# A convolution ahead of a feed-forward: seven pairs of rounds convolved beside TensorE instead of six, and seven half tasks on GpSimd instead of four

## The chip, the cores and the metric

The kernel runs on one core of a Trainium2 chip. The metric is device time in microseconds (us) of one execution; lower is better. The engines are TensorE (PE, matrix products; PEld is its weight loads), VectorE (DVE), ScalarE (ACT), GpSimd (POOL) and SyncE (SP, which only issues transfers here).

## What is computed

The input x is 8 sequences of 3904 rows of 192 numbers. First comes a causal convolution along the sequence: 8 heads of 24 columns, 7 taps for each head, the taps a softmax of `weight`. Its result, 31232 rows, goes through a product of two linear maps and two more linear maps:

```python
out = np.einsum('hk,bskhg->bshg', w, x_unf)      # w: softmax of the taps, x_unf: 7 shifted rows
a = x @ w1                                        # (31232,192) @ (192,1024)
b = x @ w2
h = a * b @ w3                                    # (1024,1024)
return (h @ w_out).astype(np.float32)             # (1024,192)
```

## The kernel before

**Two streams and rounds.** The rows are cut into two halves of 15616 (`TS`), which are worked side by side: partitions 0 to 63 hold 64 columns of one half, 64 to 127 of the other. A half is cut into 31 rounds of 512 rows (the last has 256). The last two maps are multiplied once at the start (`w3_product`, L651), so each round has two products. The first (`first_product`, L543) makes a and b for 8 slices of 128 columns, 24 matmuls a slice (L558), reading the convolved rows transposed (columns on partitions); ACT copies a out of PSUM (`asb`, L565), and DVE multiplies it by b into `abT` (L567). The second (`second_product`, L577, once for each half) is 32 matmuls (L583), a copy by ACT (L588) and one output transfer on SP's queue (L593).

**Phases.** Rounds are taken in threes. Phase 0 has the second products of rounds 0 to 2 (their first products are the prologue); phase p from 1 to 8 has the first products of rounds 3p to 3p + 2 and then their six second products. Phase 9 takes the first products of 27 to 29, phase 10 the rest. A phase's places 0 to 5 are the points behind its six second products.

**Two ways to convolve.** Most rounds are convolved on PE. Rows are loaded in windows of 32, of which 26 come out (`conv`, L306, matmuls L324 with a band of taps, evicted by ACT or DVE at L333). Windows are gathered in blocks (`SIZES`): four in the prologue, then 40, 80, 80, 80. A block's x comes by casting loads on GpSimd's queue (L158), four for 40 windows, eight or more for 80, more where a sequence starts inside. A unit is one `conv` call over all windows of a block and part of its columns: a block of 40 is two units of 64 matmuls, a block of 80 four units of 32. `places` tells behind which second product of which phase each unit stands. With its last unit, the block is stored to DRAM (`store`, L355 and L362, on SP's queue) and read back transposed, round by round, three DMA transposes each (`transposes`, L396), into a ring of four rounds (`xT`).

The rounds of the pairs in `SIDE` are convolved beside PE. Pair p is rounds 2p + 1 and 2p + 2. For each 64 columns (a task, three to a pair) GpSimd's queue casts the rows into DRAM (`side_cast`, L440), SP's queue brings them in transposed (`side_transpose`, L450), ACT writes the tap next to the last (`side_first`, L456), and DVE adds the other six, one operation over 1024 columns each (`side_sums`, L474). Where a sequence starts inside a task, five of these six are cut in two. Two whole tasks, named in `BY_POOL`, are summed by GpSimd in halves of 512 columns instead (`pool_sums`, L501 to L521, with its own transpose, L495).

**What sets the order.** It is written out by hand, and each engine works its own instructions in order. The DVE sums are dealt over the phases by a count (`room`: 9 in phase 0, then 12) and stand behind the last `abT` of their phase, beside the second products. GpSimd's loads, casts and sums are dealt to eight `points` in the first products of a phase; each point first waits for one slice of `abT` (`pace`, L811). Each transfer on GpSimd's queue waits for the landing of the one eight places ahead of it; on SP's queue too. At the end of a phase come the transposes of rounds that are due up to two phases on; the side's transposes for the next phase stand behind the first products. Side pairs write in turn to two tiles.

Of the kernel before, what the change touches and what calls it, by code (L numbers as in the profile page):

```python
# [16 lines left out]
def kernel(  # L17
# [14 lines left out]
    G = D // H  # L32
# [6 lines left out]
    CH = 512  # L39
    NR = -(-TS // CH)  # L40
    RING = 4 * CH
    LAG = 2
    TRIO = LAG + 1
    Q = 64
    NP = D // Q
    C = 32
    ST = C - PAD
    LAG_ROWS = (LAG + 1) * CH
    SIDE = (3, 6, 7, 10, 11, 14)
    SIZES = [20, 20, 20, 40, 40, 80, 80, 80]  # L50
    NB = len(SIZES)
    FIRST = [sum(SIZES[:b]) for b in range(NB)]
    XN = 20 * D
# [359 lines left out]
    def side_span(p):  # L413
        return (2 * p + 1) * CH, min((2 * p + 3) * CH, TS)

    BY_POOL = ((7, 2), (11, 2))
    tasks = [(q, k) for q in SIDE for k in range(NP) if (q, k) not in BY_POOL]
    side_of, acc_of, raw_of = {}, [], []
    RAW = HALO + 2 * CH

# [11 lines left out]
                "p (k t) -> p k t", k=NP)  # L432

    def side_cast(i, task=None):
        p, k = task or tasks[i]
        t0, t1 = side_span(p)

        def job(r):
            def run():
                nc.gpsimd.dma_start(  # L440
                    out=rows_c[t0 - HALO:t1, k, r * Q:r * Q + Q],
                    in_=x_rows[r * TS + t0 - HALO:r * TS + t1, k * Q:k * Q + Q])
            return run
        return [job(r) for r in range(NS)]

    def side_transpose(i):
        p, k = tasks[i]
        t0, t1 = side_span(p)
        for lo, hi in ((t0 - HALO, t0 + CH), (t0 + CH, t1)):
            nc.sync.dma_start_transpose(  # L450
                out=raw_of[i % 5 - 1][:, HALO + lo - t0:HALO + hi - t0], in_=rows_c[lo:hi, k, :])

    def side_first(i):
        p, k = tasks[i]
        t0, t1 = side_span(p)
        nc.scalar.activation(  # L456
            out=acc_of[i % 2][:, 0:t1 - t0], in_=raw_of[i % 5 - 1][:, HALO - 1:HALO - 1 + t1 - t0],
            func=ACT.Copy, scale=wC[:, k, K - 2:K - 1])

    def side_sums(i):  # L460
        p, k = tasks[i]
        t0, t1 = side_span(p)
        starts = [z for z in range(0, TS, S) if t0 <= z < t1]

        def job(d, last):
            def run():
                raw, acc = raw_of[i % 5 - 1], acc_of[i % 2]
                if d == 2:
                    for z in starts:
                        nc.vector.memset(acc[:, z - t0:z - t0 + 1], 0.0)  # L470
                for lo, hi in [(t0, t1)] if last else \
                        zip([t0] + [z + d for z in starts], starts + [t1]):
                    a = acc[:, lo - t0:hi - t0]
                    nc.vector.scalar_tensor_tensor(  # L474
                        out=side_of[p][:, k, 0:t1 - t0] if last else a,
                        in0=raw[:, HALO + lo - t0 - d:HALO + hi - t0 - d],
                        scalar=wC[:, k, K - 1 - d:K - d], in1=a, op0=ALU.mult, op1=ALU.add)
# [9 lines left out]
        pool_raw.append(t[:, 2 * CH:3 * CH + HALO])  # L487

    def pool_half(p, k, half):
        lo = side_span(p)[0] + half * CH  # L490
        return p, k, lo, [z for z in range(0, TS, S) if lo <= z < lo + CH]

    def pool_transpose(p, k, half):
# [191 lines left out]
    def stage_of(R):  # L685
        return R // TRIO

    places = {0: (0, 1), 1: (0, 1, 3, 4), 2: (2, 4), 3: (1, 3), 5: (2, 4), 6: (1, 3)}
    starts, chain, room, p = {}, {}, 0, -1
    for i, (q, k) in enumerate(tasks):  # L690
        for cost, f in side_sums(i):
            while room < cost:
                p += 1
                room = 9 if p == 0 else 12
                at, ends = 0, {}
                starts.setdefault(p, [])
            if not chain or chain[max(chain)][-1][0] != i:
                starts[p].append(i)
                n = max(p == 0, -(-ends.get(i - 2, 0) // 2))
                chain.setdefault(p, []).append((i, n, lambda i=i: side_first(i)))  # L700
            assert p < stage_of(2 * q + 1)
            room, at = room - cost, at + cost
            chain.setdefault(p, []).append((i, None, f))
        ends[i] = at
    for p in starts:
        for i in starts[p]:
            assert i < 5 or p < 2 or max(v for v in chain if chain[v][0][0] <= i - 5) <= p - 2

    def side_steps(p, n, state):
        items = chain.get(p, [])  # L710
# [17 lines left out]
    def later_loads():  # L728
        nc.gpsimd.tensor_scalar(out=taps, in0=taps, scalar1=total, scalar2=None, op0=ALU.mult)
        load_x(3)  # L730
        load_wo()
        load_w3(4, 2)
        load_w3(6, 2)
        for i in starts[0]:
            for f in side_cast(i):
                f()
        load_x(4)
        for i in starts[1] + starts[2]:
            for f in side_cast(i):
                f()  # L740

# [14 lines left out]
        4: seq((w3_product, 4), (w3_product, 6),  # L756
               (conv, 3, 96, 96, (A,), (0,)), (conv, 3, 96, 96, (V,), (1,)),
               (A, wC[Q:128], wC[0:Q]), (side_tiles,), *[(side_transpose, i) for i in starts[0]],
               (store, 3), (transposes, 3))})


    units = [(b, h, n) for b in range(4, NB)
# [2 lines left out]
    assert sum(map(len, places.values())) == len(units)  # L765
    points = ((0, 1), (0, 4), (0, 7), (1, 2), (1, 5), (2, 0), (2, 3), (2, 6))
    jobs = {p: [] for p in range(1, len(phases))}
    for p, b, part in ((1, 5, 0), (1, 5, 1), (2, 6, 0), (2, 6, 1), (4, 7, 0), (5, 7, 1)):
        jobs[p] += x_jobs(b, part)
    pool_at = {2: 3, 3: 4, 4: 7, 5: 7, 6: 7}  # L770
    halves = [(q, k, h) for q, k in BY_POOL for h in range(2)]
    pool_sum = [f for v in halves for f in pool_sums(*v)]
    assert sum(pool_at.values()) == len(pool_sum)
    pool_from = {1: halves[0], 3: halves[1], 4: halves[2], 5: halves[3]}
    casts = [(p - 1, f) for p in starts if p > 2 for i in starts[p] for f in side_cast(i)]
    casts += [(p, f) for p, t in zip((1, 4), BY_POOL) for f in side_cast(None, t)]
    casts.sort(key=lambda c: c[0])
    for p in jobs:
        due_now = sum(d <= p for d, _ in casts)
# [1 line left out]
        first = [] if p == 1 else [f for _, f in casts[:due_now]]  # L781
        jobs[p] = first + jobs[p] + [f for _, f in casts[len(first):ahead]]
        del casts[:ahead]
    sent = [LAG + 2]
    due = []

    def convolve(p):
        b, h, n = units.pop(0)
        conv(b, h * G, n * G, (V, A) if p not in chain else (A, A))
        if h + n == H:  # L790
            store(b)
            while sent[0] < len(conv_rounds) and \
                    min((conv_rounds[sent[0]] + 1) * CH, TS) <= spans[b - 3][1]:
                due.append(conv_rounds[sent[0]])
                sent[0] += 1
            if p == 0:
                while stage_of(due[0]) <= 1:
                    transposes(due.pop(0))

    pace = const.tile([1, 2], BF16)  # L800
    for p, (rounds, ends) in enumerate(phases):
        todo = jobs.pop(p, [])

        each = -(-len(todo) // len(points))
        at = [[todo.pop(0) for _ in range(min(each, len(todo)))] for _ in points]
        for v in {0: (), 3: (1, 3, 5), 4: (0, 2, 4, 6), 7: range(7)}[pool_at.get(p, 0)]:
            at[v].append(pool_sum.pop(0))
# [12 lines left out]
        for b in list(zero_rows):  # L820
            for xb, p0, w in zero_rows.pop(b):
                nc.gpsimd.memset(xb[p0:p0 + PAD, w, :], 0.0)
        if p == 0:
            pool_tiles()
        for i in starts.get(p + 1, ()) if p else ():
            side_transpose(i)
        if p in pool_from:
            pool_transpose(*pool_from[p])
        state = set()
        side_steps(p, 0, state)  # L830
        for n, (R, r) in enumerate((R, r) for R in ends for r in range(NS)):
            (last_product if (R, r) == (NR - 1, NS - 1) else second_product)(R, r)
            if p == 0:
                side_steps(p, n + 1, state)
            if n in places.get(p, ()):
                convolve(p)
            side_steps(p, n + 1, state)
        assert len(state) == len(chain.get(p, ()))
        while due and stage_of(due[0]) <= p + 2:
            transposes(due.pop(0))  # L840
# [33 lines left out]
```

## Time and profile before

| what | value |
|---|---|
| median of three runs | 514.49 us (513.63 to 517.32) |
| the profiled execution | 514.11 us, of which 512.4 us span |
| `abT` on DVE (L567) | 240 of 1221 ns |
| `asb` on ACT (L565) | 244 of 1012 ns |
| sums on DVE (L474), 1024 columns | 1283 ns |
| first tap on ACT (L456), 1024 columns | 1160 ns |
| GpSimd's product (L501) and sum (L521), 512 columns | 1568 and 1266 ns |
| `ops` of a second product (L583) | 1936 matmuls, 164.0 us |
| `cps` of the convolution (L324) | 832 matmuls, 10.8 us |
| x loads on GpSimd's queue, 240 KB | 28, 7.4 us to landing |
| casts on GpSimd's queue, 130 KB | 30, 6.9 us to landing |

Busy times are sums over one execution and overlap between engines. Matmuls on PE are pipelined, four or two of them side by side on parts of the array, so their times added up exceed what they take; the chain of work gives what a group takes. The view of DMA queues calls GpSimd's queue q0 and SP's q1; both feed the same 16 DMA engines.

### The profile page before, as it was taken

The numbers are of one execution on the slowest core, as the hardware profiler recorded it, in microseconds if no ns is written. First come the engines' busy times: TensorE is split into PE (matmuls) and PEld (weight loads), VectorE is DVE, ScalarE is ACT, GpSimd is POOL, SyncE is SP. The second block draws the span as 40 slices with busy tenths as digits, with TensorE's granted clock in tenths as the row PEclk, the third lists the DMA queues.
The fourth block names the chain that finished last, engine by engine and source line by source line (L and its number), as shares of the span: only waits on it lengthen the run. The fifth ranks groups of instructions, "written<-read, shape, count | busy, mean of one in ns | idle before, by whom it ended". The sixth has DMA issues, their size and how long they took to land.

```text
span 512.4 us, 13886 instructions
## 1 busy us (share of the span) xinstructions
PE 506.9 (99%) x5892; PEld 341.0 (67%) x5892; DVE 432.5 (84%) x430; ACT 351.6 (69%) x397; POOL 161.4 (31%) x232
## 2 busy tenths in 40 slices
PE   9999999999999999999999999999999999999997
PEld 4446875496569557855875596569557845874597
DVE  7798779997999899999999998999899899339930
ACT  6786757778775876777657757776776477357742
POOL 9876004201750364069408911960000000000000
PEclk9999999999999999999999999999999999999999
DMA  9999979997999565799659534404841420230025
GB/s 142 146 170 161 166 176 195 179 174 140 178 153 204 107 50 33 178 175 161 105 146 136 65 107 101 47 11 133 156 84 33 152 66 0 71 117 1 1 64 155
DMA packets 154134, 59.45 MB, mean 116 GB/s; under 512 B 108891, under 2 KB 154071, under 8 KB 154071
## 3 DMA queue, kind: packets, MB, share of 16 engines
q1 hardware_dynamic: 86999, 41.39, 37.8%
q0 software_dynamic: 66912, 17.07, 36.5%
q8 instruction: 46, 0.75, 0.6%
q14 instruction: 17, 0.14, 0.1%
q10 hardware_dynamic: 160, 0.10, 0.1%
HBM read 34.42 MB, written 34.88 MB: 135 GB/s over the span
## 4 chain that ended last, share of the span: by engine, by line
PE 94%; ACT 2%; POOL 1%; DMA 1%; DVE 1%; issue 1%; ACTq 0%; POOLq 0%
PE ops L583 31%; PE pa L558 30%; PE pb L558 30%; DMA xb<-in_x_dram 1%; PE cps L324 1%; PE wps L651 1%; ACT convo L333 1%; ACT asb L565 1%; DVE abT L567 0%; ACT acc L456 0%; POOL xb L158 0%; PE ops L604 0%; POOL wn L226 0%; POOL wn L227 0%; POOL wn L228 0%
## 5 line engine op out<-in xcount | busy, mean ns | idle before, releaser
L567 DVE TENSOR_TENSOR abT<-asb,pb 128x1024 bf16<-128x1024 bf16 x240 | 292.7, 1221 | 50.6 <-ACT asb L565 35.1
L565 ACT CAST asb<-pa 128x1024 bf16<-128x1024 f32 x244 | 247.0, 1012 | 64.3 <-PE pa L558 63.9
L558 PEld LDWEIGHTS <-wn 64*128 64x128 bf16 x1488 | 138.5, 94 | 79.8 <-issue 1.4
L558 PEld LDWEIGHTS <-ws 64*128 64x128 bf16 x1488 | 129.5, 94 | 69.3 <-issue 1.6
L583 PE MATMUL ops<-W_sb,abT 128*128 128x192 bf16 x1936 | 164.0, 246 | 0.2 <-ACT convo L333 0.2
L583 PEld LDWEIGHTS <-abT 128*128 128x128 bf16 x1936 | 158.5, 98 | 6.7 <-issue 6.6
L558 PE MATMUL pb<-xT,wn 64*128 64x512 bf16 x456 | 124.4, 376 | 0.0
L558 PE MATMUL pa<-xT,wn 64*128 64x512 bf16 x456 | 123.1, 376 | 0.2
L558 PE MATMUL pa<-xT,ws 64*128 64x512 bf16 x456 | 123.1, 376 | 0.0
L558 PE MATMUL pb<-xT,ws 64*128 64x512 bf16 x456 | 121.1, 376 | 0.0
L588 ACT COPY osb<-ops 128x768 f32<-128x768 f32 (+1 forms) x61 | 48.5, 795 | 84.0 <-PE ops L583 82.2
L474 DVE SCALAR_TENSOR_TENSOR acc<-raw,wC,acc 128x320 f32<-128x320 bf16 (+4 forms) x90 | 76.2, 894 | 0.7
L558 PE MATMUL pb<-side,wn 64*128 64x512 bf16 (+1 forms) x288 | 75.7, 367 | 0.0
L558 PE MATMUL pa<-side,ws 64*128 64x512 bf16 (+1 forms) x288 | 74.4, 367 | 0.0
L558 PE MATMUL pa<-side,wn 64*128 64x512 bf16 (+1 forms) x288 | 74.4, 367 | 0.0
L558 PE MATMUL pb<-side,ws 64*128 64x512 bf16 (+1 forms) x288 | 72.9, 367 | 0.0
L811 POOL COPY pace<-abT 1x2 bf16<-1x2 bf16 x44 | 7.7, 174 | 159.2 <-DVE abT L567 159.1
L501 POOL TENSOR_SCALAR tmp<-acc,wC 128x512 f32<-128x512 bf16 x24 | 37.6, 1568 | 0.8
L333 ACT CAST convo<-cps 128x640 bf16<-128x640 f32 (+2 forms) x58 | 33.8, 661 | 2.1 <-PE cps L324 2.1
L158 POOL DMA_DIRECT2D xb<-in_x_dram x46 | 31.0, 677 | 4.1 <-issue 3.5
L440 POOL DMA_DIRECT2D rows_c<-in_x_dram x36 | 28.1, 783 | 9.5 <-issue 4.1
L521 POOL TENSOR_TENSOR acc<-acc,tmp 128x512 f32<-128x512 f32 (+6 forms) x25 | 26.0, 1047 | 1.7
(72 smaller groups left out, 172.4 us busy)
## 6 DMA issues: line engine op xcount, KB each, us to landing
out_dram<-osb SPq DMA_DIRECT2D x54, 384.0 KB
xb<-in_x_dram POOLq DMA_DIRECT2D x28, 240.0 KB, 7.4
rows_c<-in_x_dram POOLq DMA_DIRECT2D x30, 130.0 KB, 6.9
out_dram<-osb SPq DMA_DIRECT2D x12, 192.0 KB
rows<-convo SPq DMA_DIRECT2D x9, 240.0 KB
xb<-in_x_dram POOLq DMA_DIRECT2D x8, 228.0 KB, 8.0
rows<-convo SPq DMA_DIRECT2D x9, 150.0 KB
w3b<-in_moe_w_dram POOLq DMA_DIRECT2D x4, 256.0 KB, 5.6
```

The costliest lines, as they stand in the source:

```text
L158: nc.gpsimd.dma_start(out=tiles[js[0]][0][group(r, e), s:s + w, :], in_=bass.AP(tensor=x.tensor, offset=(r * TS + t - PAD) * D, ap=[[D, C] ...
L333: f(out=convo[:, e::E, k, :, lo:lo + c] .rearrange("p w r g -> p r w g"), in_=src[:, :, :, o:o + c])
L440: nc.gpsimd.dma_start(out=rows_c[t0 - HALO:t1, k, r * Q:r * Q + Q], in_=x_rows[r * TS + t0 - HALO:r * TS + t1, k * Q:k * Q + Q])
L474: nc.vector.scalar_tensor_tensor(out=side_of[p][:, k, 0:t1 - t0] if last else a, in0=raw[:, HALO + lo - t0 - d:HALO + hi - t0 - d], scalar ...
L501: nc.gpsimd.tensor_scalar(out=out, in0=pool_raw[0][:, HALO - d:HALO - d + CH], scalar1=wC[:, k, K - 1 - d:K - d], scalar2=None, op0=ALU.mult)
L521: nc.gpsimd.tensor_tensor(out=a, in0=a, in1=tmp[:, lo - t0:hi - t0], op=ALU.add)
L558: nc.tensor.matmul(p[:, r, f * N:f * N + N], w_of(i, k, r)[rs, ft * 128:(ft + 1) * 128], operand(R, k, rs), start=(k == 0), stop=(k == NP ...
L565: nc.scalar.copy(out=asb[:, :, 0:per * N], in_=pa[:, :, 0:per * N])
L567: nc.vector.tensor_tensor(out=ab[:, f0, :, 0:N], in0=asb[:, :, 0:N], in1=pb[:, :, 0:N], op=ALU.mult)
L583: nc.tensor.matmul(ops[:, g // 2, (g % 2) * D:(g % 2) * D + D], ab[:, jt, r, g * 128:(g + 1) * 128], W_sb[:, jt, :], start=(jt == 0), stop ...
L588: nc.scalar.copy(out=osb.rearrange("p (a g) d -> p a (g d)", g=2), in_=ops[:, 0:ng // 2, 0:2 * D])
L811: P(out=pace, in_=abT_of[R][0:1, ft, 1, 0:2])
```

## The change

The pairs beside PE become 4, 5, 8, 9, 12, 13 and 14 in place of 3, 6, 7, 10, 11 and 14: seven pairs, 14 rounds. The blocks after the prologue are three of 80. The first of them (rounds 5 to 8) is convolved in phase 0, at places 1 to 4, the second (rounds 13 to 16) in phases 2 and 3, the third (rounds 21 to 24) in phases 4 and 5. Sequence starts now lie in rounds that PE convolves, so no task is cut in two, and loads of x are. Seven half tasks go to GpSimd, one in each of phases 2 to 8; a task may keep half on DVE. DVE's counts become 9, four times 11, four times 12, and its sums reach into phase 8. In phase 0 the two first taps of ACT stand at places 1 and 4, no longer both at 1. All x of the first block of 80 is loaded in the prologue, ahead of four casts; before, it was a block of 40 ahead of eight. The transposes of round 4 move up behind those of round 3, and `turn` sends the transposes of a round once the round that held its place in the ring has been read. Outside phase 0 it is called before the side's transposes and at the end of the phase. PE's matmuls for the two products are the same; its convolution has 704 matmuls.

```diff
-    SIDE = (3, 6, 7, 10, 11, 14)
-    SIZES = [20, 20, 20, 40, 40, 80, 80, 80]
+    SIDE = (4, 5, 8, 9, 12, 13, 14)
+    SIZES = [20, 20, 20, 40, 80, 80, 80]
...
-    BY_POOL = ((7, 2), (11, 2))
-    tasks = [(q, k) for q in SIDE for k in range(NP) if (q, k) not in BY_POOL]
+    BY_POOL = ((5, 2, 0), (5, 2, 1), (8, 2, 0), (8, 2, 1), (12, 2, 0), (12, 2, 1), (13, 2, 0))
+    tasks = []
+    for q in SIDE:
+        for k in range(NP):
+            left = [h for h in range(2) if (q, k, h) not in BY_POOL]
+            if left:
+                tasks.append((q, k, half_of(q, left[0])[0], half_of(q, left[-1])[1]))
...
-    places = {0: (0, 1), 1: (0, 1, 3, 4), 2: (2, 4), 3: (1, 3), 5: (2, 4), 6: (1, 3)}
+    places = {0: (1, 2, 3, 4), 2: (1, 3), 3: (0, 1), 4: (2, 4), 5: (1, 3)}
+    rooms = (9, 11, 11, 11, 11, 12, 12, 12, 12)
...
-                room = 9 if p == 0 else 12
+                room = rooms[p]
...
-                n = max(p == 0, -(-ends.get(i - 2, 0) // 2))
+                n = max((p == 0) * (3 * len(starts[p]) - 2), -(-ends.get(i - 2, 0) // 2))
...
         load_x(4)
-        for i in starts[1] + starts[2]:
+        for i in starts[1]:
             for f in side_cast(i):
                 f()
...
-               (store, 3), (transposes, 3))})
+               (store, 3), (transposes, 3), (transposes, 4))})
...
-    for p, b, part in ((1, 5, 0), (1, 5, 1), (2, 6, 0), (2, 6, 1), (4, 7, 0), (5, 7, 1)):
+    for p, b, part in ((1, 5, 0), (2, 5, 1), (3, 6, 0), (4, 6, 1)):
         jobs[p] += x_jobs(b, part)
...
+    pool_from = {p: v for p, v in enumerate(BY_POOL, 1)}
+    pool_sum = {p + 1: pool_sums(*v) for p, v in pool_from.items()}
...
-    sent = [LAG + 2]
+    sent = [LAG + 3]
...
-        conv(b, h * G, n * G, (V, A) if p not in chain else (A, A))
+        conv(b, h * G, n * G, (V, A) if p not in chain or (p == 0 and h == 2 * n) else (A, A))
...
+    def turn(p):
+        while due and stage_of(due[0]) <= p + 2 and \
+                stage_of(conv_rounds[ring_of[due[0]] - RING // CH]) <= p:
+            transposes(due.pop(0))
...
-        for i in starts.get(p + 1, ()) if p else ():
-            side_transpose(i)
+        turn(p)
+        raws = starts.get(p + 1, ())
+        late = [i for i in raws if p == 0 or i >= 5 and chain[p][0][0] <= i - 5]
+        for i in raws:
+            if i not in late:
+                side_transpose(i)
...
-        while due and stage_of(due[0]) <= p + 2:
-            transposes(due.pop(0))
-        for i in starts[1] if p == 0 else ():
+        turn(p)
+        for i in late:
             side_transpose(i)
```

More of the change, by code (lines that the diff above doesn't have):

```diff
@@ L414, in side_span, with half_of @@
         return (2 * p + 1) * CH, min((2 * p + 3) * CH, TS)
-    BY_POOL = ((7, 2), (11, 2))
-    tasks = [(q, k) for q in SIDE for k in range(NP) if (q, k) not in BY_POOL]
+    def half_of(q, h):
+        t0, t1 = side_span(q)
+        return t0 + h * CH, min(t0 + h * CH + CH, t1)
+    BY_POOL = ((5, 2, 0), (5, 2, 1), (8, 2, 0), (8, 2, 1), (12, 2, 0), (12, 2, 1), (13, 2, 0))
[5 more added lines that the diff above has]
+                tasks.append((q, k, half_of(q, left[0])[0], half_of(q, left[-1])[1]))
     side_of, acc_of, raw_of = {}, [], []
@@ L434, in side_cast @@
     def side_cast(i, task=None):
-        p, k = task or tasks[i]
-        t0, t1 = side_span(p)
+        p, k, t0, t1 = task or tasks[i]
         def job(r):
@@ L446, in side_transpose @@
     def side_transpose(i):
-        p, k = tasks[i]
-        t0, t1 = side_span(p)
-        for lo, hi in ((t0 - HALO, t0 + CH), (t0 + CH, t1)):
+        p, k, t0, t1 = tasks[i]
+        for lo, hi in ((t0 - HALO, t0 + CH), (t0 + CH, t1))[:1 + (t1 - t0 > CH)]:
             nc.sync.dma_start_transpose(
@@ L453, in side_first @@
     def side_first(i):
-        p, k = tasks[i]
-        t0, t1 = side_span(p)
+        p, k, t0, t1 = tasks[i]
         nc.scalar.activation(
@@ L460, in side_sums @@
     def side_sums(i):
-        p, k = tasks[i]
-        t0, t1 = side_span(p)
+        p, k, t0, t1 = tasks[i]
         starts = [z for z in range(0, TS, S) if t0 <= z < t1]
+        o = t0 - side_span(p)[0]
         def job(d, last):
@@ L474, in run @@
                     nc.vector.scalar_tensor_tensor(
-                        out=side_of[p][:, k, 0:t1 - t0] if last else a,
+                        out=side_of[p][:, k, o:o + t1 - t0] if last else a,
                         in0=raw[:, HALO + lo - t0 - d:HALO + hi - t0 - d],
@@ L489, in pool_half @@
     def pool_half(p, k, half):
-        lo = side_span(p)[0] + half * CH
+        lo = half_of(p, half)[0]
         return p, k, lo, [z for z in range(0, TS, S) if lo <= z < lo + CH]
@@ L686, in stage_of @@
         return R // TRIO
-    places = {0: (0, 1), 1: (0, 1, 3, 4), 2: (2, 4), 3: (1, 3), 5: (2, 4), 6: (1, 3)}
+    places = {0: (1, 2, 3, 4), 2: (1, 3), 3: (0, 1), 4: (2, 4), 5: (1, 3)}
+    rooms = (9, 11, 11, 11, 11, 12, 12, 12, 12)
     starts, chain, room, p = {}, {}, 0, -1
-    for i, (q, k) in enumerate(tasks):
+    for i, (q, *_) in enumerate(tasks):
         for cost, f in side_sums(i):
@@ L706 @@
         for i in starts[p]:
-            assert i < 5 or p < 2 or max(v for v in chain if chain[v][0][0] <= i - 5) <= p - 2
+            assert i < 5 or p < 2 or max(v for v in chain if chain[v][0][0] <= i - 5) <= p - 1
     def side_steps(p, n, state):
@@ L767 @@
     jobs = {p: [] for p in range(1, len(phases))}
-    for p, b, part in ((1, 5, 0), (1, 5, 1), (2, 6, 0), (2, 6, 1), (4, 7, 0), (5, 7, 1)):
+    for p, b, part in ((1, 5, 0), (2, 5, 1), (3, 6, 0), (4, 6, 1)):
         jobs[p] += x_jobs(b, part)
[L770 to L776, printed above, removed]
+    pool_from = {p: v for p, v in enumerate(BY_POOL, 1)}
+    pool_sum = {p + 1: pool_sums(*v) for p, v in pool_from.items()}
+    casts = [(p - 1, f) for p in starts if p > 1 for i in starts[p] for f in side_cast(i)]
+    casts += [(p, f) for p, (q, k, h) in pool_from.items()
+              for f in side_cast(None, (q, k, *half_of(q, h)))]
     casts.sort(key=lambda c: c[0])
@@ L796, in convolve @@
             if p == 0:
-                while stage_of(due[0]) <= 1:
-                    transposes(due.pop(0))
+                turn(0)
+    def turn(p):
+        while due and stage_of(due[0]) <= p + 2 and \
+                stage_of(conv_rounds[ring_of[due[0]] - RING // CH]) <= p:
+            transposes(due.pop(0))
     pace = const.tile([1, 2], BF16)
@@ L805 @@
         at = [[todo.pop(0) for _ in range(min(each, len(todo)))] for _ in points]
-        for v in {0: (), 3: (1, 3, 5), 4: (0, 2, 4, 6), 7: range(7)}[pool_at.get(p, 0)]:
-            at[v].append(pool_sum.pop(0))
+        for v, f in enumerate(pool_sum.pop(p, ())):
+            at[v].append(f)
         def issue(R, ft, fs):
@@ L832 @@
             (last_product if (R, r) == (NR - 1, NS - 1) else second_product)(R, r)
-            if p == 0:
-                side_steps(p, n + 1, state)
             if n in places.get(p, ()):
@@ L838 @@
         assert len(state) == len(chain.get(p, ()))
-        while due and stage_of(due[0]) <= p + 2:
-            transposes(due.pop(0))
-        for i in starts[1] if p == 0 else ():
+        turn(p)
+        for i in late:
             side_transpose(i)
```

## The prediction

> **What bounds the kernel now.** I read the page first, then busy time by stretch, then the chain of work, then the queues. TensorE (PE) is busy 506.9 of 512.4 us:
>
> ```profile
> PE 506.9 (99%) x5892; PEld 341.0 (67%) x5892; DVE 432.5 (84%) x430; ACT 351.6 (69%) x397; POOL 161.4 (31%) x232
> ```
>
> By stretches of 10 us it loses time only before 70 us; from there each shows 10.00 of 10.00, at a granted clock of 1.00. So time goes where PE work goes, and comes where PE is made to wait. The chain over phase 1 prices a unit of a block of 80 (32 matmuls): 0.35 us between second products.
>
> ```profile
> 105.17 0.35 PE cps L324 x32
> 105.53 2.75 PE ops L583 x32
> 108.27 0.35 PE cps L324 x32
> ...
> 120.21 0.75 PE pa L558 x6
> ```
>
> Phases start in the chain at 71.24, 120.21, 168.33, 216.44, 263.63, 311.74, 359.85, 407.04 and 454.18. Phases without units (263.63 less 216.44, 407.04 less 359.85) take 47.19, with two 48.11, with four 48.97: a unit costs 0.46 all in, and phases are rigid.
>
> In phase 0 ScalarE's two first taps stand before the evictions of the 40-block's units, and PE waits:
>
> ```profile
> 56.34 1.11 ACT acc L456
> 57.50 1.15 ACT acc L456
> 58.65 1.83 ACT convo L333 x4
> ```
>
> GpSimd's queue, by time, at the loads of block 4 and the casts behind them:
>
> ```profile
> 39.06 2.72 POOL L158 DMA_DIRECT2D xb<-in_x_dram  x4 [1.19 <-issue]
> ...
> 49.85 0.76 POOL L440 DMA_DIRECT2D rows_c<-in_x_dram  x1 [1.55 <-DMA xb<-in_x_dram]
> 52.18 0.76 POOL L440 DMA_DIRECT2D rows_c<-in_x_dram  x1 [1.56 <-DMA xb<-in_x_dram]
> ```
>
> The last casts each wait for the landing of the DMA eight places ahead. SP's queue, where a block of 80 goes to DRAM and back transposed (columns: start, us, ...):
>
> ```profile
> 356.69 10.40 SPq L362 DMA_DIRECT2D rows<-convo  x8
> 367.14 0.90 SPq L355 DMA_DIRECT2D rows<-convo  x1
> 368.13 1.74 SPq L593 DMA_DIRECT2D out_dram<-osb  x2
> 369.97 9.05 SPq L396 DMA_TRANSPOSE xT<-rows  x6
> ```
>
> Storing 80 windows takes 11.4 us on an otherwise quiet queue. The DMA view of 136 to 142 us and of 78.5 to 81 us shows what GpSimd's loads (q0) do to SP's (q1):
>
> ```profile
> q0 software_dynamic: 1165, 0.43, 79.0%
> q1 hardware_dynamic: 1651, 0.43, 74.8%
> ```
>
> and
>
> ```profile
> q0 software_dynamic: 1050, 0.40, 140.5%
> q1 hardware_dynamic: 30, 0.01, 1.7%
> ```
>
> **The sum, part by part**, against the profiled execution (514.11 us: its span and 1.7 around it, which stay; 0.4 below the median of 514.49).
>
> (a) Units after 71 us: twelve become eight, four in phase 1 gone: 4 x 0.46 = -1.8.
>
> (b) Phase 0: 52.79 to 71.24 is 18.45: six second products at 2.69 (5.39 for two) are 16.14, two units at 0.67 are 1.34, waits 0.97. After: 16.14 + 4 x 0.46 = 17.98, since the two first taps are now at places 1 and 4, with a unit's evictions (about 1.9) and one result copy (0.80) inside 3.15 us of PE each, as phase 1 shows without a wait. -0.5. Phase 1 then starts at 70.8.
>
> (c) Block 4 is 80 windows: twelve x loads for four, with eight places between each and the one it waits for, so the last is issued at 52.2, where the last cast was. Its convolution comes after two second products, at 52.79 + 5.4 = 58.2. A 168 KB load lands 3.9 us after issue when alone (DMA issues), that cast 12.9 after: ends 56.1 and 65.1, a wait of 0 to 6.9. The rows are the same, the queue ahead is 0.8 MB, so the median of block 4's loads (7.5) is nearer above and 3.9 below: about 58.2 with the edge memset, wait 0.5. It folds into (d): what PE waits here, round 5 needn't.
>
> (d) Round 5 (its xT comes from block 4) is PE's third in phase 1: 70.8 + 2 x 10.36 = 91.5. Block 4's last eviction ends at 52.79 + 5 x 2.69 + 4 x 0.46 + 2.24 = 70.3 (2.24 from 117.46 to 119.70, unit to store, in phase 1), and SP has round 4's transposes and five outputs ahead. Low end: the quiet row, 356.69 to three transposes issued at about 374.9 less 1.7 for outputs, 16.5 + 1 to land (estimate; the shortest x load takes 2.0 with its issue): 87.8, no wait. High end: six transposes end at 59.09 + 2 x 4.49 = 68.1, five outputs at 1.37 (0.75 MB in 2.7 us) end at 75.0; then the contended row, 119.70 to the third transpose's last packets at 142, less one output, plus 1: 22 more, 97: a wait of 5.4. Block 5's loads are issued at the points where before's were (76.6, 80.1), so q1 meets the second DMA row above; I lean to the high end: (c)+(d) = +3.0.
>
> By the Trainium skill, DMA: Bandwidth & Descriptors, section Queues, rings and completion order, each DMA engine takes turns between queue rows packet by packet. The second DMA row (1050 packets to 30, with transposes issued and waiting) disagrees; by the rule SP would lose half of those 2.5 us, and (d) would be 1.8.
>
> (e) Round 13 (block 5) is PE's second in phase 4, at P4 + 10.4 (P4: that phase's start). Block 5's last unit is at place 1 of phase 3, whose unit ends 37.4 after the phase's start (108.62 less 71.24); + 2.24, so its store begins at P4 - 8.5 (48.11 less 39.6). Behind it SP has four outputs (two in the quiet row), then round 13's three transposes. Quiet: 18.2 + 2 x 1.37 + 1 = 21.9: P4 + 13.4, a wait of 3.0. Contended: 22.3 + 3 x 1.37 + 1 = 27.4: P4 + 18.9, a wait of 8.5. Casts in phase 4 reach the queue at about P4 + 7, as at 127 us, so the store is quiet and outputs and transposes are not: +5.5. Before, no block had this deadline: the one stored in phase 1 was first read in phase 3.
>
> Costed at nothing: vector sums 9, 11 to 12 a phase at 1.285, without splits (15.4, where chains of 15.96 ended 1.58 into the next phase without loss); the halves on GpSimd (18.5 us of sums a phase, beside first products, as in phases 4 to 6); the larger phase 8 chain (16 x 1.02 = 16.3), beside 16.1 of second products; its cover gone, each would cost its excess. One cast in phase 1 waits for a late transpose; nothing else of that phase is behind it on GpSimd.
>
> The Trainium skill, SBUF — State Buffer, section Who interferes with whom, has a vector operation with two SBUF inputs blocked by a GpSimd operation that reads SBUF. That would bind where GpSimd's last sums overlap the vector sums. The products that GpSimd mostly runs beside have one PSUM input and show no effect: 21 in 24.58 us with GpSimd busy 21.4 of 26, and in 24.59 with it idle. One blocked operation of 1.57 us stays within the slack above, so the sum is the same; a row of them is in the last rival.
>
> Sum: 514.1 - 1.8 - 0.5 + 3.0 + 5.5 = **520.3 us**, 1.1% over the median.
>
> **Rivals.**
> 1. *The transposed rows arrive in time* and the convolution's saving is what is left: 514.1 - 2.3 = 511.8. This decides if store, outputs and transposes together take under 18.9 us for round 13. For: no transposed operand is waited for over 0.2 us now. Against: the quiet row alone has 21.9.
> 2. *Only round 13 is late*, round 5 slips through: 511.8 + 0.5 + 5.5 = 517.8. For: from 70 to 80 us the DMA engines move only 118 GB/s, so there is room. Against: the outputs moved ahead of the store fill it.
> 3. *Both at their contended ends*: 511.8 + 5.4 + 8.5 = 525.7.
> 4. *Phase 0 waits for x as long as the last cast took* (6.9), or GpSimd's halves hold up vector sums in each of seven phases (up to 1.57 each, 11): with (e), 522 to 528.
>
> **How the numbers follow.** Forecast 0.40 (518.5 to 522.5), rivals 0.15, 0.25, 0.12, 0.08. The range of 513.0 to 525.5 leaves out most of rival 1 and half of rivals 3 and 4, about 0.2. About 1% is what a measurement here can tell from no change: slower means above 519.6, faster below 509.3. Above 519.6: three quarters of the forecast's case (0.30), rival 3, most of 4, a tenth of 2: 0.50. Faster 0.03, for a gain no row shows; the rest, 0.47, within 1%.
>
> **What would show it.** PE waits in only three places past 52 us: at the first unit of phase 0 (for x loads or the memset), at round 5 and at round 13 (for xT); phases 1, 6, 7 and 8 without these 47.2 long, phases 2, 3 and 5 48.1. PE's convolution has 704 matmuls, not 832. I'm wrong if phase 4 is 48.1 long, or if SP's round 13 transposes are issued before P4 + 5.

## The result

The changed kernel takes 539.78 us (median; 539.59 to 540.27), the kernel before 514.26 beside it (513.63 to 517.32): 4.8% slower, ratio 1.0483, 95% interval 1.0457 to 1.0510. The forecast was 520.3, its range ended at 525.5. The profiled execution has a span of 538.2 us.

The page of the changed kernel, busy time and the row of the granted clock (40 slices of 13.5 us):

```profile
PE 512.4 (95%) x5764; PEld 342.5 (64%) x5764; DVE 444.7 (83%) x396; ACT 348.8 (65%) x389; POOL 230.6 (43%) x301
...
PEclk9999889789999999996999999999999999999999
```

PE's share falls from 99% to 95%, and three dents stand in a clock that was 1.00 throughout before. The matmuls are 128 fewer, as the diff says (704 of the convolution for 832).

Phases read from PE's instructions, before, as forecast, and after:

| phase | before | forecast | after |
|---|---|---|---|
| 0 (second products) | 18.4 | 18.0 + 0.5 | 25.1 |
| 1 | 48.97 | 47.2 + 2.5 | 58.0 |
| 4 | 48.1 | 48.1 + 5.5 | 58.1 |
| 2, 3, 5 | 48.1, 48.1, 48.1 | 48.1 each | 48.1 each |
| 6, 7 | 47.2 each | 47.2 each | 47.2 each |

All of the loss is in the three phases that were named. 511.8 (the sum with nothing late) + 7.1 + 10.8 + 10.0 = 539.7. The waits of the changed kernel (us in total, times, longest) name what is late:

```profile
POOL rows_c L448 <- DMA raw<-rows_c: 16.6, 1, 16.6
PE pa L564 <- DMA xT<-rows: 16.0, 3, 8.6
...
ACT acc L462 <- DMA side<-rows_c: 7.4, 1, 7.4
...
PE cps L324 <- ACT osb L594: 4.4, 1, 4.4
```

PE's 16.0 are rounds 5 and 13. Its 4.4 stand at the second unit of phase 0, and they are not for x: the last x load had landed at 57.45, and the first unit ran at 57.97 without a wait.

```profile
57.97 0.43 PE L324 MATMUL cps<-xb,Aband 32*32 32x240 bf16 x32
58.33 2.81 PE L589 MATMUL ops<-W_sb,abT 128*128 128x192 bf16 x32
65.51 0.38 PE L324 MATMUL cps<-xb,Aband 32*32 32x240 bf16 x2 [4.37 <-ACT osb L594]
```

ScalarE's first tap waits 7.4 for a transpose, and the copy of the second result, which frees PE's bank, is behind it:

```profile
55.44 0.80 ACT L594 COPY osb<-ops 128x768 f32<-128x768 f32 x1 [2.58 <-PE ops L589]
63.63 1.15 ACT L462 ACTIVATE acc<-side,wC 128x1024 f32<-128x1024 bf16 x1 [7.39 <-DMA side<-rows_c]
64.68 0.78 ACT L594 COPY osb<-ops 128x768 f32<-128x768 f32 x1
```

The chain leads from that tap back to a cast on GpSimd:

```profile
53.05 2.30 POOL rows_c L448 x3
55.35 5.55 DMA rows_c<-in_x_dram
...
60.96 2.56 DMA side<-rows_c
...
63.63 1.15 ACT acc L462
```

Pairs 4 and 5 are now neighbours. The cast for the first task of pair 5 writes the 16 halo rows ahead of its span, and these are the last 16 rows that the second transpose of pair 4's first task reads, in the same DRAM tensor `rows_c`. (Both pairs' casts write the same values into these rows, so the order changes nothing but the time.) That cast stands behind block 4's twelve x loads and lands at 60.9, so SP, which issues in order, stands still from 45.4 to 60.9. Its queue by time:

```profile
44.12 17.96 SPq L457 DMA_TRANSPOSE side<-rows_c  x2
62.20 2.50 SPq L457 DMA_TRANSPOSE raw<-rows_c  x2
64.80 4.93 SPq L362 DMA_DIRECT2D rows<-convo  x8
...
70.34 8.68 SPq L396 DMA_TRANSPOSE xT<-rows  x6
79.06 4.45 SPq L599 DMA_DIRECT2D out_dram<-osb  x5
83.61 10.40 SPq L362 DMA_DIRECT2D rows<-convo  x6
```

Block 3's store, the transposes of rounds 3 and 4 and five results are pushed back with it, and block 4's store is first issued at 83.61, where the forecast had 75.0 at the contended end. Its last row leaves SP at 99.46, round 5's first transpose at 100.11.

Round 13, on the other hand, is as forecast in kind. The store, its results and its transposes:

```profile
223.48 7.69 SPq L362 DMA_DIRECT2D rows<-convo  x6
...
235.04 1.40 SPq L355 DMA_DIRECT2D rows<-convo  x1
236.54 4.25 SPq L599 DMA_DIRECT2D out_dram<-osb  x4
240.89 10.09 SPq L396 DMA_TRANSPOSE xT<-rows  x6
```

Phase 4 starts at 231.85: the store begins 8.4 ahead (forecast 8.5) and takes 13.0 where the quiet row had 11.4, the four results 4.25 (two in the quiet row and two at 1.37 make 4.5), and PE goes on with the last of the three transposes at 250.9, 10.0 after the first was issued. No cast runs beside the store, since GpSimd issues its first one of the phase at 236.57; casts run beside the results and the transposes.

What was not foreseen is the clock. Windows of the changed kernel around the three waits (us from the start: length, then busy time and instructions of PE, PEld, DVE, ACT and POOL, PEclk, DMA share, GB/s):

```profile
63.60:70.20 6.60, 3.97 (x51) 3.14 (x51) 5.25 (x5) 6.10 (x9) 0.00 (x0) 0.50 0.73 132
101.00:111.20 10.20, 4.08 (x20) 1.59 (x22) 1.11 (x1) 1.01 (x1) 0.00 (x0) 0.50 1.23 160
244.40:254.60 10.20, 4.83 (x22) 1.77 (x24) 1.22 (x1) 1.54 (x2) 5.17 (x6) 0.50 1.29 160
```

PE's clock is halved 2.0 to 2.5 us after each pause begins and stays halved until after work is back: 4.8 (4.1 without the gaps in it), 4.2 and 3.8 us at half speed. By this, about 2.0, 2.1 and 1.9 us are lost (an estimate: half of the work in these stretches).

### The profile page after: what moved, and what is told of

Same layout as the page of the kernel before. It is cut to its first block, busy times and chain, and to the rows that moved or that the text cites. A ratio compares the mean times of both kernels' runs of the same rounds, so it can differ in the third digit from the quotient of the medians.

```text
span 538.2 us, 13687 instructions
## 1 busy us (share of the span) xinstructions
PE 512.4 (95%) x5764; PEld 342.5 (64%) x5764; DVE 444.7 (83%) x396; ACT 348.8 (65%) x389; POOL 230.6 (43%) x301
## 4 chain that ended last, share of the span: by engine, by line
PE 77%; DMA 11%; POOL 4%; DVE 3%; SPq 1%; ACT 1%; issue 1%; POOLq 0%; ACTq 0%; DVEq 0%
PE ops L589 26%; PE pa L564 25%; PE pb L564 25%; DMA xb<-in_x_dram 3%; DVE acc L480 2%; DMA rows_c<-in_x_dram 2%; DMA xT<-rows 2%; DMA rows<-convo 2%; POOL xb L158 1%; POOL ws L220 1%; POOL w3b L638 1%; DMA wn<-in_moe_w_dram 1%; SPq L362 1%; PE cps L324 1%; SPq L396 1%
## 5 line engine op out<-in xcount | busy, mean ns | idle before, releaser
L564 PEld LDWEIGHTS <-wn 64*128 64x128 bf16 x1488 | 138.9, 95 | 96.1 <-DMA xT<-rows 15.9
L564 PE MATMUL pb<-xT,wn 64*128 64x512 bf16 x408 | 113.6, 381 | 0.0
L564 PE MATMUL pb<-xT,ws 64*128 64x512 bf16 x408 | 110.3, 381 | 0.1
L564 PE MATMUL pb<-side,wn 64*128 64x512 bf16 (+1 forms) x336 | 88.9, 368 | 0.1
L564 PE MATMUL pa<-side,wn 64*128 64x512 bf16 (+1 forms) x336 | 87.3, 369 | 0.0
L564 PE MATMUL pa<-side,ws 64*128 64x512 bf16 (+1 forms) x336 | 87.3, 369 | 0.0
L480 DVE SCALAR_TENSOR_TENSOR acc<-raw,wC,acc 128x1024 f32<-128x1024 bf16 (+2 forms) x70 | 85.1, 1216 | 2.5 <-ACT acc L462 0.5
L564 PE MATMUL pb<-side,ws 64*128 64x512 bf16 (+1 forms) x336 | 85.6, 368 | 0.0
L507 POOL TENSOR_SCALAR tmp<-acc,wC 128x512 f32<-128x512 bf16 x42 | 65.9, 1568 | 1.2
L448 POOL DMA_DIRECT2D rows_c<-in_x_dram x50 | 38.0, 763 | 22.2 <-DMA raw<-rows_c 16.6
L527 POOL TENSOR_TENSOR acc<-acc,tmp 128x512 f32<-128x512 f32 x35 | 44.4, 1268 | 2.9
L480 DVE SCALAR_TENSOR_TENSOR acc<-side,wC,acc 128x1024 f32<-128x1024 bf16 (+1 forms) x20 | 25.2, 1261 | 11.2 <-ACT acc L462 10.7
```

What stands on the lines that cost most here:

```text
L448: nc.gpsimd.dma_start(out=rows_c[t0 - HALO:t1, k, r * Q:r * Q + Q], in_=x_rows[r * TS + t0 - HALO:r * TS + t1, k * Q:k * Q + Q])
L480: nc.vector.scalar_tensor_tensor(out=side_of[p][:, k, o:o + t1 - t0] if last else a, in0=raw[:, HALO + lo - t0 - d:HALO + hi - t0 - d], sc ...
L507: nc.gpsimd.tensor_scalar(out=out, in0=pool_raw[0][:, HALO - d:HALO - d + CH], scalar1=wC[:, k, K - 1 - d:K - d], scalar2=None, op0=ALU.mult)
L527: nc.gpsimd.tensor_tensor(out=a, in0=a, in1=tmp[:, lo - t0:hi - t0], op=ALU.add)
L564: nc.tensor.matmul(p[:, r, f * N:f * N + N], w_of(i, k, r)[rs, ft * 128:(ft + 1) * 128], operand(R, k, rs), start=(k == 0), stop=(k == NP ...
```

## The experiments

Phase lengths of each kernel, from its profiled execution, beside its measured ratio to the kernel before:

| kernel | median us | ratio, 95% interval | phase 0 | phase 1 | phase 4 |
|---|---|---|---|---|---|
| after | 539.78 | 1.0457 to 1.0510 | 25.1 | 58.0 | 58.1 |
| e1_two_tensors | 533.05 | 1.0285 to 1.0373 | 25.0 | 51.5 | 58.5 |
| e2_block5_early | 529.27 | 1.0213 to 1.0297 | 24.6 | 58.4 | 48.1 |
| e3_both | 524.05 | 1.0126 to 1.0198 | 25.6 | 51.5 | 48.1 |
| e4_casts_first | 535.00 | 1.0345 to 1.0443 | 28.3 | 49.2 | 58.4 |
| e5_fill13 | 537.04 | 1.0364 to 1.0486 | 24.8 | 58.1 | 55.9 |
| e6_store_late | 524.50 | 1.0125 to 1.0210 | 20.7 | 55.2 | 48.1 |
| e7_loads_late | 519.09 | 1.0048 to 1.0097 | 26.1 | 47.1 | 48.1 |
| e8_both_late | 525.28 | 1.0148 to 1.0240 | 18.9 | 58.5 | 48.1 |
| e9_freed | 524.71 | 1.0147 to 1.0228 | 25.2 | 53.9 | 48.1 |
| e10_freed_early | 523.57 | 1.0090 to 1.0214 | 22.2 | 53.3 | 48.1 |
| e11_in_time | 519.64 | 1.0045 to 1.0103 | 25.4 | 47.1 | 48.1 |

**e1_two_tensors**: the shared halo rows taken away.

```diff
-    rows_c = dram.tile([TS, NP, NS * Q], BF16, name="rows_c")
+    rows_2 = [dram.tile([TS, NP, NS * Q], BF16, name=f"rows_c{i}") for i in range(2)]
...
+    def rows_of(q):
+        return rows_2[SIDE.index(q) % 2]
...
```

> The side pairs' rows go to two DRAM tensors, taken in turn, so that the casts of pair 5 no longer share 16 halo rows with the transposes of pair 4; nothing else moves. Theory (the second transpose of task 0 waits for the casts of pair 5 behind twelve x loads, and holds ScalarE's first tap and all of SP's queue): phase 0 is 18 to 19.5 long instead of 25.1, GpSimd's wait of 16.6 and the tap's wait of 7.4 are gone, round 5's xT comes 3 to 9 us earlier; phase 4 stays at 58. Total 521 to 529. Rival (block 4's x loads are what is late): phase 0 stays at 24 to 25, total within 2 us of 539.8. Rival (SP's queue is long in any case): phase 0 is short, but round 5's wait moves with it and stays at 9 or more, total 531 to 534.

6.7 us came back; the theory had 11 to 19 (521 to 529). GpSimd's wait of 16.6, ScalarE's of 7.4 and SP's standstill are gone, and block 4's store moves from 83.61 to 77.34:

```profile
43.45 2.52 SPq L460 DMA_TRANSPOSE side<-rows_c  x2
46.67 3.15 SPq L460 DMA_TRANSPOSE raw<-rows_c  x2
49.99 7.84 SPq L362 DMA_DIRECT2D rows<-convo  x8
...
60.40 8.16 SPq L396 DMA_TRANSPOSE xT<-rows  x6
68.60 7.39 SPq L602 DMA_DIRECT2D out_dram<-osb  x5
77.34 7.84 SPq L362 DMA_DIRECT2D rows<-convo  x6
```

Phase 1 is 6.4 shorter. But phase 0 is as long as it was, as the first rival had it (the total is in the range of the second, which had expected a short phase 0). One wait has made room for another: with SP's queue at work again, the last x load lands at 63.36 instead of 57.45, and PE's first unit now waits for x itself:

```profile
PE cps L324 <- DMA xb<-in_x_dram: 3.5, 2, 2.0
```

**e2_block5_early**: the last units of block 5 moved to phase 2.

```diff
-    places = {0: (1, 2, 3, 4), 2: (1, 3), 3: (0, 1), 4: (2, 4), 5: (1, 3)}
+    places = {0: (1, 2, 3, 4), 2: (0, 1, 3, 4), 4: (2, 4), 5: (1, 3)}
```

> The last two units of block 5 move from phase 3 to phase 2, so that its store and the transposes of round 13 are issued a phase earlier; phase 0 is as in the changed kernel. Theory (round 13's xT was late because the store stands 8.5 us before phase 4, behind it outputs and casts): phase 4 is 48.1 long instead of 58.1 and its clock stays at 1.0, phase 2 is 49.0, phase 3 47.2: total 529.5 to 531. Rival (the transposes are slow beside other transfers wherever they stand): PE still waits over 2 us for xT in phase 4, total 533 or more.

As the theory said, and a little better: 529.27, phase 4 at 48.1 and phase 2 at 49.3. Of PE's waits for xT one is left, 9.0. Term (e) was about the deadline: a phase earlier, the same store and transposes are in time.

**e3_both**: the two edits together.

> Both edits: two DRAM tensors and block 5 convolved in phase 2. Theory: the two gains add up (phase 0 and round 5: 11 to 18; phase 4: 10): total 512 to 519; 512 if round 5's xT comes in time, which would be the rival of the prediction that all transposes come in time. Rival (the waits hide each other): total over 521.

524.05: over 521, as the rival had it, but not for its reason. The gains nearly add up (10.5 and 6.7 make 17.2, measured 15.7); the first is smaller than the theory had it, since phase 0 stays. The DMA queues from 50 to 57 us show what x now shares the engines with. In the changed kernel, where SP stands still:

```profile
q0 software_dynamic: 3930, 1.17, 158.2%
q1 hardware_dynamic: 98, 0.02, 2.4%
```

and in e3_both, where SP transposes and stores beside:

```profile
q0 software_dynamic: 1737, 0.63, 84.2%
q1 hardware_dynamic: 1795, 0.45, 63.8%
```

(packets, MB, time as a share of the span of 16 engines). GpSimd's queue moves 0.63 MB in place of 1.17, and the last x load lands at 63.94 instead of 57.45, issued 1.2 later.

**e4_casts_first**: the casts ahead of the x loads, halo rows still shared.

```diff
-        load_x(4)
         for i in starts[1]:
             for f in side_cast(i):
                 f()
+        load_x(4)
```

> GpSimd issues the casts of phase 1's side tasks ahead of block 4's twelve x loads instead of behind them; the shared halo rows stay. Theory (the late casts are the cause): the second transpose of task 0 issues 6 to 9 us earlier, phase 0 gets 3 to 6 shorter, although x comes 3 to 5 us later, round 5's wait shrinks as much, phase 4 stays at 58: total 526 to 534. Rival (the x loads are what PE waits for): the same loads come later, so the first unit waits longer and the total is 540 to 545.

535.00, between the two. Phase 0 went the rival's way (28.3, 3.2 longer, PE's first unit waits for x), phase 1 the theory's (49.2, 8.8 shorter). SP's second transpose was issued at 48.67 instead of 60.96, and the last x load landed at 63.66 instead of 57.45. So both accounts hold, each in its phase.

**e5_fill13**: matmuls of zeros in the wait for round 13.

```diff
+            if R == 13:
+                warm(28)
             first_product(R, {ft: issue(R, ft, at[v])
```

> The changed kernel with 28 matmuls of zeros (128x512, no result used) ahead of round 13's first product, where TensorE waits 6.7 us; they fill 6.0 us at full clock. Theory (TensorE's pause lowers the granted clock to 0.5 for 10.24 us, and the part of it that outlasts the wait costs about 2): the clock in phase 4 stays at 1.0, xT comes no earlier, phase 4 goes from 58.1 to 55.5 to 56.7, total 537 to 538.5. Rival (the clock is no cost, or the wait alone sets the phase's end): phase 4 within 0.5 of 58.1, total within 0.7 of 539.8; or longer, if the filling matmuls outlast the wait.

The windows of the kernel with the filling:

```profile
240.00:244.00 4.00, 4.00 (x31) 1.82 (x28) 3.78 (x4) 2.42 (x3) 3.43 (x5) 1.00 1.63 274
244.00:248.00 4.00, 4.00 (x20) 1.84 (x19) 0.24 (x1) 0.00 (x0) 3.89 (x6) 1.00 2.23 192
248.00:252.00 4.00, 2.87 (x22) 1.06 (x22) 0.00 (x0) 0.92 (x1) 1.82 (x2) 1.00 1.51 199
252.00:256.00 4.00, 4.00 (x40) 2.11 (x38) 3.66 (x3) 3.13 (x4) 0.00 (x1) 1.00 0.64 82
```

The clock stays at 1.00, round 13's product starts as late as before, and phase 4 is 55.9: 2.3 less. The interval of the whole time (ratio 1.0364 to 1.0486) is too wide to show so little; the phase shows it. So this wait costs its length and about 2 more. For the other two waits that is read from the rows of the clock alone, without a run that fills them.

**e6_store_late, e7_loads_late, e8_both_late**: on e3_both, block 3's store with the transposes of rounds 3 and 4 moved behind phase 0's first result (e6), phase 1's loads and casts issued at the last 5 of 8 points only (e7), and both (e8).

```diff
-               (A, wC[Q:128], wC[0:Q]), (side_tiles,), *[(side_transpose, i) for i in starts[0]],
-               (store, 3), (transposes, 3), (transposes, 4))})
+               (A, wC[Q:128], wC[0:Q]), (side_tiles,), *[(side_transpose, i) for i in starts[0]])})
...
+            if (p, n) == (0, 0):
+                store(3)
+                transposes(3)
+                transposes(4)
...
-        each = -(-len(todo) // len(points))
+        free = range(3 if p == 1 else 0, len(points))
+        each = -(-len(todo) // len(free))
```

> Two tensors and block 5 in phase 2, and block 3's store with the transposes of rounds 3 and 4 issued behind the first result of phase 0 instead of ahead of it, so that SP's queue is quiet until about 56 us. Theory (with the shared rows gone, block 4's x loads share the DMA engines with SP's store and transposes and land at 63.9 instead of 57.5; phase 0 waits for that): the last x load lands at 57 to 59, phase 0 is 18 to 20 instead of 25.6, unless round 3's own xT is then late by up to 3; round 5's wait stays at 3 to 6 with its clock: total 516 to 521. Rival (x is late by its own bytes, or by the casts): last x load lands after 62, total within 2 of 524.

> Two tensors and block 5 in phase 2, and GpSimd's x loads and casts of phase 1 issued from the second round's middle on (5 of the 8 points) instead of from the first round on. Theory (block 4's store and round 5's transposes are stretched by those loads): the store, 12.9 us long from its first issue, takes 10 to 11.5, round 5's wait of about 2.7 with its half clock shrinks, phase 1 goes from 51.5 to 48 to 50, unless phase 2's first taps or units are then late; phase 0 stays at 25 to 26: total 520.5 to 523. Rival (SP's own queue is the length): store 12.5 or more, total within 1 of 524.

> The two edits together. Theory: phase 0 18 to 20, phase 1 48 to 51, all others as they are: total 513 to 518, near the kernel before. Rival (moved transfers collide with those behind them, as the first tap did with the x loads): over 520.

e6: phase 0 falls from 25.6 to 20.7 and the last x load lands at 60.98, the theory's way but short of its 57 to 59, and the total doesn't move (524.50, the rival's): phase 1 gives it all back. e8 is the clearest of the set. Its phase 0 is 18.9, as its theory had it and near the forecast's 18.5, but its phase 1 is 58.5, as long as without any edit, and its total is the rival's (525.28). SP's queue in e8:

```profile
56.77 6.39 SPq L362 DMA_DIRECT2D rows<-convo  x8
...
65.08 8.18 SPq L396 DMA_TRANSPOSE xT<-rows  x6
73.31 3.24 SPq L602 DMA_DIRECT2D out_dram<-osb  x4
76.64 9.21 SPq L362 DMA_DIRECT2D rows<-convo  x6
...
90.28 11.13 SPq L396 DMA_TRANSPOSE xT<-rows  x6
```

Block 4's store is first issued at 76.64 here, at 77.44 in e6, at 77.34 in e1 and 77.72 in e3, wherever phase 0 ended; round 5 waits from there. So in these four phases 0 and 1 together take 75.9 to 77.3, while phase 0 alone goes from 18.9 to 25.6. The equal times have two causes. In e1 and e3 SP is free and waits for the eviction of block 4's last unit, which late x has put back. In e6 and e8 x is earlier, but SP's queue is full: the store and transposes that the edit put behind the first result, and four results after them, take SP until 76.55 in e8.

SP issues nothing from 50 to 56 us in e6, but its queue isn't quiet on the DMA engines: the four side transposes issued before move nearly as much there as all of SP's transfers did in e3_both. From 50 to 57 us, e6:

```profile
q0 software_dynamic: 1728, 0.63, 85.2%
q1 hardware_dynamic: 1745, 0.42, 62.8%
```

In the changed kernel only the first of these four could run ahead of 61 us.

e7 came out better than its theory: round 5's wait vanishes, phase 1 is 47.1, the total 519.09. The store is hardly shorter (12.0 for 12.8, where 10 to 11.5 was expected), and SP issues round 5's first transpose no earlier (90.39 for 90.58 in e3); it is their landing that GpSimd's loads had held up: e3's PE goes on with the last at 102.1, e7's needs them from 99.5 and doesn't wait. In e8 the same edit doesn't help: phase 1 starts 7.3 earlier there than in e7, so PE needs round 5 earlier, and GpSimd's loads, tied to the first products, start at 88.11 and run beside round 5's transposes. In e7 they start at 95.43, when the third of these is being issued.

**e9_freed, e10_freed_early, e11_in_time**: the casts for phase 1's tasks issued in phase 1 (e9, e10), and phase 0's results sent to DRAM only behind block 4's store and the transposes of rounds 5 and 6 (all three; in e11 all but the first, and the casts where they were). In e9 and e10, with no result ahead of it, block 3's store is issued at about 50; in e11 it waits for the first result. The main lines of e9's edit:

```diff
+            if R < TRIO:
+                held.append((out[t0:t0 + n * 128, :], osb[:, g:g + n, :]))
+                continue
...
-    casts = [(p - 1, f) for p in starts if p > 1 for i in starts[p] for f in side_cast(i)]
+    casts = [(p - 1, f) for p in starts if p > 0 for i in starts[p] for f in side_cast(i)]
```

> The kernel with both late edits (block 3's store behind phase 0's first result, phase 1's loads late), and two things taken out of the way of block 4: the casts for phase 1's side tasks are issued in phase 1 instead of behind block 4's x loads, and phase 0's six results go to DRAM behind block 4's store and the transposes of rounds 5 and 6 instead of between. Theory (block 4 passes x load, store and transposes one after another, and what stands in SP's queue and on the DMA engines beside it makes round 5's xT late; in the kernel with both late edits the store was first issued at 76.6, 5 after phase 0's end): store from 70 to 73.5, round 5's wait from 9.9 to 0 to 4, phase 0 18 to 19.5, phase 1 47.2 to 53, total 512.5 to 518. Rival (block 4's own bytes take that long whatever is beside them): round 5's xT comes no more than 2 us earlier, total over 521.

> The same two things taken away, but block 3's store ahead of phase 0's results, as in the changed kernel, so that it runs beside the x loads. Theory: with the casts gone the x loads land at 58 to 61 instead of 64, phase 0 is 18.5 to 22 instead of 26; block 4's store starts at 70 to 75, so round 5's wait is 0 to 4: total 513 to 518. Rival (store 3 and the transposes are what slow x, not the casts): phase 0 stays at 25 to 26, and total at 518 to 520.

> The kernel with both late edits, whose phase 0 was 18.9 long but whose round 5 waited 9.9 because SP issued block 4's store only at 76.6; now five of phase 0's six results go to DRAM behind block 4's store and the transposes of rounds 5 and 6, and the casts stay in the prologue. Theory (block 4's way is a chain of x loads, store and transposes; each stretch of it that runs without company on SP's queue and on the DMA engines is short enough, none of them beside another is): x lands near 59, the store is first issued at 73 to 74 and takes 12.3, round 5's third transpose is issued by 89 to 90.5, its wait is 0 to 2.5, phase 1 47.2 to 51, total 513 to 517, as the kernel before or up to 0.5% over it. Rival (the deferred results or the transposes behind them make a new wait in phase 1's second products, as the late casts did): phase 1 over 51.5, total over 518.

In none of the three does PE wait for round 5, but all miss the totals of their theories and none beats the kernel before. e9 (524.71) and e10 (523.57) run into a new wait: the casts now come late for the taps of phase 1. The waits of e9:

```profile
ACT acc L465 <- DMA raw<-rows_c: 12.8, 2, 12.5
```

This holds ScalarE's result copies, and PE its second products (4.1, and the clock after it). e9 also shows the store alone: GpSimd's queue moves nothing from 77 to 89 us, and from 77.18 to 89.39 it takes 12.2 us. With 11.4 in the kernel before and 13.0 for block 5 in the changed kernel, a store beside which GpSimd's queue moves nothing takes 11.4 to 13.0; e3's 12.8 is no more than that, e8's 13.6 and the changed kernel's 15.9 are. Its place in the queue counts for more. In e11 (519.64) round 5 is in time and the casts too, but x lands at 62.67, phase 0 is 25.4, and the total is 0.5 to 1.0% over the kernel before. It missed its 513 to 517 by that, and by 1.1 more in phase 2.

## Why the prediction was wrong, step by step

- (a) and (b), the units: right. Phases 6 and 7 are 47.2, phases 2, 3 and 5 48.1, to 0.1, and e8's phase 0 comes to 18.9 with x nearly in time (forecast 18.0 + 0.5).
- "Costed at nothing": DVE's sums, GpSimd's halves, phase 8 and the longer chains cost nothing that shows, since those phases have their forecast lengths. Rival 4's halves are out. What the working left out stands next to its sentence on the cast in phase 1 that waits for a late transpose: that wait, 16.6 us on GpSimd, does cost nothing that shows, but the same overlap of halo rows works the other way in the prologue, where a transpose waits for a cast and SP's queue behind it. The prediction priced the order of each queue and not what pairs 4 and 5 share.
- (c) and (d), "+3.0": this is the step that failed. Measured 17.9 (7.1 and 10.8), of which about 4.1 is clock, so 13.8 of waits. (d) had SP's queue at work all through phase 0, with block 4's store at 75.0 at the latest; SP stood still from 45.4 to 60.9 for the overlapping cast, and the store began at 83.61. e1 shows that the shared rows carry 6.7 of the loss.
- (c)'s own number came true, by luck: it had x ready at about 58.2, a wait of 0.5, and the last load landed at 57.45. That holds only while SP stands still. With the shared rows gone x lands at 63.4 (e1) and 63.9 (e3), near (c)'s upper end of 65.1, and round 5's xT is behind a store that begins at 77, so most of the loss stays, in e1 as in e3. The median that (c) took was that of four loads at the head of this queue, while the last cast's 12.9 was measured at its end, with SP's transfers beside it, and was the nearer row for a kernel whose SP is at work.
- Two of the three places were named for a wrong reason, then: phase 0 lost its time at the second unit, for a result copy, and not at the first for x or the memset; round 5 was late mostly by a standstill that no term has (PE's waits there are 8.6 in the changed kernel and 2.2 in e1).
- (d) also said "what PE waits here, round 5 needn't". In e1, e3, e6 and e8 phases 0 and 1 do add up to nearly the same, but by two causes (late x in the first two, SP's full queue in the others), and in e7 they make 73.2. Block 4's way is x loads, units, store and transposes, each of which can be the late one, so the two ends could not be chosen one by one.
- The Trainium skill, DMA: Bandwidth & Descriptors, section Queues, rings and completion order, has each DMA engine take turns between queues packet by packet. In the prediction a row of 1050 packets to 30 spoke against it; in e3_both's window, where x is late, q0 and q1 share at 1737 to 1795, which agrees with the rule in the sum over 7 us. So both rows occur, and the rule was the better guide to what the x loads lose.
- (e), "+5.5": right in its mechanism (e2), too small. Of the 10.0 in phase 4, 8.1 are waits and 1.9 is clock (e5 gives 2.3 for it). From the store's first issue to PE's going on it took 27.4, which is the contended end's 27.4; the term was taken between the two ends because the store would be quiet, and the quiet store took 13.0 for 11.4.
- The clock is in no term. By the estimate above, about 6.0 of the 19.5 us between forecast and result are lost to half speed after the three waits.

What stays open: the last x load lands at 59.0 in e8, 61.0 in e6 and 62.7 in e11, though they issue it within 1.4 us of each other. In 50 to 57 us GpSimd's queue moves 0.81, 0.63 and 0.62 MB in them. e6 and e8 issue the same instructions up to phase 1, so 2 us of this is scatter between executions, and differences of that size in one phase 0 settle nothing. Not tried: issuing the side transposes later, and shrinking block 4 itself.

## What to carry to other kernels

When a change makes two tasks neighbours, look for the rows that they share in DRAM: here a read waited for an overlapping write ahead of it in the program, and in phase 1 a write for a read, and an in-order queue passed the wait on to everything behind. Price a late transfer as a chain to the deadline that it feeds, because work moved along that chain can make the next link late (e6, e8), and transfers set free by one wait's removal can make another (e1). A long wait of the matmul engine can cost more than its length, by the half-speed stretch behind it (e5).

## What the runs showed of the hardware

After the long pauses of PE (3.2 us and more) in these runs, the granted clock falls to 0.50 some 2.0 to 3.1 us after the pause begins. The low stretches are 3.4, 6.8 or 10.2 us long; in the changed kernel the clock comes back 3.8 to 4.8 us after work resumes. It does not take one long pause. In e3_both, phase 0 has a pause of 2.0 us, 0.6 us of matmuls, and a second pause, 0.3 us into which the clock falls:

```profile
58.00:61.00 3.00, 0.72 (x10) 0.11 (x9) 2.93 (x3) 0.80 (x1) 1.60 (x4) 1.00 1.42 227
61.20:67.80 6.60, 4.20 (x43) 3.39 (x44) 3.85 (x3) 1.82 (x2) 0.00 (x0) 0.50 1.82 156
```

In its phase 1, pauses of 1.1 and 0.8 us close together are followed by 3.4 us at 0.50. Pauses of 1.6 and 0.6 us in e6's phase 0 and one of 1.0 us in e11 leave the clock at 1.00, so the length of a pause alone doesn't decide it.

The Trainium skill, TensorE: Matmul & The Clock Gate, Part 1 (The HAM clock gate), tells of activity windows of about 3.4 us, of which an idle one halves the clock and a busy one restores it. The lengths here, 3.4, 6.8 and 10.2, are one, two and three such windows, so the runs agree in that; that the clock fell 2.0 us into a pause, and after two short pauses with matmuls between them, goes beyond what the section says of an idle window.
